# Transposing q on VectorE from the ninth item on, and moving tiles so that both operands of a matmul start at the same address modulo 512

## The chip, the cores and the metric

The kernel runs on one core of a Trainium2 chip. The metric is the device time of one execution in microseconds. The median of three runs before the change is 977.59 us (977.21 to 977.76).

## What is computed

Linear attention with two softmaxes, then a two-layer network with the Mish activation. The batch is 8, there are 8 heads, 576 positions and a head dimension of 64; the network has 4608 tokens, width 512 and inner width 2048. All in float32.

```python
q_s = softmax(q, axis=-1)            # over the 64 elements of a row
k_s = softmax(k, axis=2)             # over the 576 positions
kv  = einsum('bhsd,bhse->bhde', k_s, v)
att = einsum('bhsd,bhde->bhse', q_s, kv)
x   = att.transpose(0, 2, 1, 3).reshape(4608, 512)
h   = x @ w_in
out = (h * tanh(log1p(exp(h)))) @ w_out
```

## The kernel before

**Items.** Attention is done in 32 items, one for each batch `b` and pair of heads `hp`; an item's two heads fill the 128 rows of TensorE. An item gives one 128x512 slab of x transposed (`xs`, features on partitions), for the first 512 of the 576 positions. The last 64 positions of all items (`xt`) go through DRAM and make a ninth column of tokens at the end.

**Slots.** The network runs in slots. Slot n takes one column of 512 tokens (`c = n // 16`) and one block of 128 inner features (`f = n % 16`). `h_mm` makes `ph` of 12 matmuls: for each of the four 128-blocks of x, the weights are stationary and x is streamed, and each product is made of three with operands split in a high and a low part (`wih`, `wil`, and x's two halves). `act` applies Mish on ScalarE (`y`) and splits the result into `gh` and `gl` on VectorE. `out_mm` comes three slots later (LAG = 3) and adds to four accumulators `po` with 12 matmuls: `gh` and `gl` are stationary and `wo` is streamed. There are 144 slots, so 1728 ph and 1728 po matmuls.

**Order.** `group(n)` writes four slots (u = 0 to 3) and puts one attention item i between them, a batch ahead of its use. At u = 1 stand `a_kv` (pkv on TensorE), `a_qscale` (row sums `qs` on VectorE, scaling of `qe` on POOL) and `a_kvs` (kvbd and its split kvr); at u = 2 `a_qt` (q transposed) ahead of `out_mm`, and behind `act` the next item's maxima (`a_max`: kmx, then qm), `a_x` (px, pxt) and `a_split` (xs); at u = 3 `a_kmax1` (pk, mxd) and `a_kmax2` (pb) for the next item. Its exponentials and the load of the one after it end the group. From slot 20 on the order on TensorE, ScalarE, VectorE and POOL is that of the code. All loads and stores are issued by SP. The first four items and the weights' preparation make a prologue; weights are still converted until about 150 us, by VectorE, ScalarE and POOL.

**q before.** `a_load` puts q's 576 rows of a head on partitions, four neighbouring rows to a partition, as 2 x 5 x 64 elements (the fifth block is the tail, held twice). The row's maximum, sum and scaling are then over 64 elements within a partition. `a_qt` transposes with five matmuls by the identity into PSUM (pq four times, pqt once). ScalarE copies pq to `qT` (for items from 8 = COLS on as the high part, with VectorE's `qTl` the low part) and pqt to `qTt`. `a_x` multiplies kv with them: three products for the 512 positions from item 8 on, one for the tail.

**Addresses.** Tiles lie in pools, in the order of their allocation; tiles named gap only take up room. In the built program the start addresses within a partition, modulo 512 bytes, are:

| tiles | role | before | after |
|---|---|---|---|
| wih, wil | stationary in ph | 192 | 64 |
| xs | streamed in ph | 64 | 64 |
| gh, gl | stationary in po | 64 | 64 |
| wo | streamed in po | 64 | 64 |
| kvrh, kvrl | stationary in px | 128 | 64 |
| qT, from item 8 on (qTh in the changed kernel) | streamed in px | 320 | 320 |
| qTl | streamed in px | 64 | 64 |

Every slice that one of these matmuls reads starts a multiple of 512 bytes behind the start of its tile.

Of the kernel before, what the change touches and what calls it, by code (L numbers as in the profile page):

```python
# [8 lines left out]
F32 = mybir.dt.float32  # L9
F32R = mybir.dt.float32r  # L10
U32 = mybir.dt.uint32
AF = mybir.ActivationFunctionType
ALU = mybir.AluOpType
AX = mybir.AxisListType
P = 128
# [7 lines left out]


@with_exitstack
def attn_mish_mlp(ctx: ExitStack, tc: tile.TileContext, q, k, v, w_in, w_out, out):

    nc = tc.nc  # L30
    B, H, S, D = q.shape
    DM, DFF = w_in.shape
    HP = H // 2
    NC = 4
    SM = NC * P
# [6 lines left out]
    NITEM = B * HP  # L42
    START = 20
    COLS = 2 * HP
    ET = mybir.EngineType

    cp = ctx.enter_context(tc.tile_pool(name="cp", bufs=1))
    lp = ctx.enter_context(tc.tile_pool(name="lp", bufs=1))
    ap = ctx.enter_context(tc.tile_pool(name="ap", bufs=1))
    xp = ctx.enter_context(tc.tile_pool(name="xp", bufs=1))  # L50
    sp = ctx.enter_context(tc.tile_pool(name="sp", bufs=4))
# [10 lines left out]
    kvbd = [pool.tile([P, P], F32, tag="kvbd", name=f"kvbd{i}") for i, pool in enumerate((pp, cp))]  # L62
    for t in kvbd:
        nc.vector.memset(t, 0.0)
    kvr = [cp.tile([P, P], F32R, tag=f"kvr{x}", name=f"kvr{x}") for x in "hl"]
    cp.tile([P, 16], F32, tag="gap", name="gap0")
    wi = [cp.tile([P, HP, DFF], F32R, tag=f"wi{x}", name=f"wi{x}") for x in "hl"]


# [3 lines left out]
    def sub(eng, out, a, b):  # L73
        eng.tensor_tensor(out, a, b, ALU.subtract)  # L74
# [68 lines left out]
    def w_end(m):  # L143

        if m < -1:
            return max(0, m + 5)
        return max(4, 2 + sum(w_due(u) <= m + 3 for u in units))

    def w_step():
        j = wstep[0]  # L150
        wstep[0] += 1
        for i, stage in ((j - 1, w_hi), (j - 2, w_lo), (j + 2, w_abs), (j + 1, w_low), (j, w_bits)):
            if 0 <= i < len(units):
                stage(units[i])
        if j + WAHEAD < len(units):
            w_load(j + WAHEAD)

    def w_until(m):
        while wstep[0] < w_end(m):
            w_step()  # L160


    at = {}
    xs = {}
    ap.tile([P, 24], F32, tag="gap", name="gap1")
    xt_dram = dp.tile([B, P, HP, ST], F32, name="xt_dram")

    vt = [p.tile([P, 2, NC + 1, D + 2], F32, tag=f"v{j}", name=f"v{j}") for j, p in enumerate((pp, pp, pp, lp))]
# [6 lines left out]
    def a_load(i):  # L175
        if i >= NITEM:
            return
        b, hp = divmod(i, HP)
        hs = slice(2 * hp, 2 * hp + 2)
        r = at[i] = {}  # L180
        for nm, src in (("k", k), ("q", q)):
            t = (pp if i < 3 else lp).tile([P, 2, NC + 1, D], F32, tag=f"{nm}{min(i, 3)}", name=f"{nm}{i}")
            nc.sync.dma_start(t[:, :, 0:NC, :], src[b, hs, 0:SM, :].rearrange("h (p c) d -> p h c d", c=NC))
            tail = src[b, hs, SM:S, :].rearrange("h p d -> p h d")
            nc.sync.dma_start(t[0:ST, :, NC, :], tail)
            nc.sync.dma_start(t[ST:P, :, NC, :], tail)
            r[nm] = t
# [20 lines left out]
    def a_max(i):  # L208
        a_kmx(i)
        a_qm(i)  # L210

    def a_qm(i):
        if i >= NITEM:
            return
        r = at[i]
        qt = r["q"].rearrange("p h c d -> p (h c) d")
        qm = ap.tile([P, 2 * (NC + 1)], F32, tag="qm", name=f"qm{i}")
        nc.vector.tensor_reduce(qm, qt, axis=AX.X, op=ALU.max)  # L218
        sub(nc.gpsimd, qt, qt, qm.unsqueeze(2).to_broadcast([P, 2 * (NC + 1), D]))

    def psum(i, tag, name):

        if i < HP and tag != "a":
            return (ps_h if tag == "h" else ps_o).tile([P, 512], F32, tag=tag, name=name)
        return ps_a.tile([P, 512], F32, tag="a", name=name)
# [20 lines left out]
    def a_exp(i, which="kq"):  # L246
        if i >= NITEM:
            return
        r = at[i]
        for nm in which:  # L250
            e = (pp if i in (0, 2) else ap).tile([P, NC + 1, 2, D], F32, tag=f"{nm}e", name=f"{nm}e{i}")
            nc.scalar.activation(e.rearrange("p c h d -> p h c d"), r[nm], AF.Exp)  # L252
            r[nm + "e"] = e

    def a_kv(i):
# [4 lines left out]
        for c in range(NC + 1):  # L260
            if i >= COLS:
                for j in range(2):
# [7 lines left out]
    def a_qscale(i):  # L270
        if i >= NITEM:
            return
        q2 = at[i]["qe"].rearrange("p c h d -> p (c h) d")
        qs = ap.tile([P, 2 * (NC + 1)], F32, tag="qs", name=f"qs{i}")
        nc.vector.tensor_reduce(qs, q2, axis=AX.X, op=ALU.add)  # L275
        nc.vector.tensor_scalar_add(qs, qs, 1e-9)
        nc.vector.reciprocal(qs, qs)  # L277
        nc.gpsimd.tensor_tensor(q2, q2, qs.unsqueeze(2).to_broadcast([P, 2 * (NC + 1), D]), ALU.mult)  # L278

    def a_kvs(i):  # L280
        if i >= NITEM:
# [6 lines left out]
        for j in range(2):  # L288
            h = slice(j * D, (j + 1) * D)
            o = 0 if i >= COLS else j * (D + 2)  # L290
            if i < HP:
                nc.scalar.activation(bd[h, h], pkv[h, o:o + D], AF.Copy, scale=rs[h])
            else:
                nc.vector.tensor_scalar_mul(bd[h, h], pkv[h, o:o + D], rs[h])
        if i >= COLS:
            nc.vector.tensor_copy(kvr[0], bd)
            sub(nc.vector, kvr[1], bd, kvr[0].bitcast(F32))

    def a_qt(i):
        if i >= NITEM:  # L300
            return
        r = at[i]
        xr = i >= COLS
        pool = pp if i in (0, 2) else ap
        qT = pool.tile([P, SM], F32R if xr else F32, tag="qT", name=f"qT{i}")
        qTt = pool.tile([P, ST], F32, tag="qTt", name=f"qTt{i}")
        pq = psum(i, "o1", f"pq{i}")
        for c in range(NC):
            nc.tensor.transpose(pq[:, c * P:(c + 1) * P], r["qe"][:, c].rearrange("p h d -> p (h d)"), ident)  # L309
        nc.scalar.copy(qT, pq)  # L310
        if xr:
            qTl = sp.tile([P, SM], F32R, tag="wc", name=f"qTl{i}")
            sub(nc.vector, qTl, pq, qT.bitcast(F32))
            r["qTl"] = qTl
        pq2 = psum(i, "o2", f"pqt{i}")
        nc.tensor.transpose(pq2[:, 0:P], r["qe"][:, NC].rearrange("p h d -> p (h d)"), ident)
        nc.scalar.copy(qTt, pq2[:, 0:ST])
        r["qT"] = qT, qTt

    def a_x(i):  # L320
# [5 lines left out]
        px = psum(i, "o3", f"px{i}")  # L326
        if i >= COLS:
            nc.tensor.matmul(px, kvr[0], qT, start=True, stop=False)  # L328
# [70 lines left out]
    def evac(c, t, copy):  # L399
        ob = pools["wp"].tile([P, DM], F32, tag="w", name=f"ob{c}_{t}")  # L400
        copy(ob, po[t])
        if c < B:
            nc.sync.dma_start(out[c * S:c * S + SM, :].rearrange("(p c) e -> p c e", c=NC)[:, t, :], ob)
        else:
            nc.sync.dma_start(out.rearrange("(b s) e -> b s e", b=B)[2 * t:2 * t + 2, SM:S, :], ob)

    def group(n):
        i = HP + n // G
        for u in range(G):
# [3 lines left out]
            if u == 0 and NITEM <= i < NITEM + HP:  # L413
                t_load(i - NITEM)
            elif u == 1:
                a_kv(i)
                a_qscale(i)
                a_kvs(i)
                v_load(i + 1)
            elif u == 2:  # L420
                a_qt(i)
            elif u == 3:
                a_kmax1(i + 1)
            if 0 <= o < NSLOT:
                out_mm(o)
                if o % NF == NF - 1:
                    for t in range(NC):
                        evac(o // NF, t, nc.scalar.copy if t >= 2 or i >= NITEM else nc.vector.tensor_copy)
# [10 lines left out]
            elif u == 3:  # L439
                a_kmax2(i + 1)  # L440
        a_exp(i + 1)
        a_load(i + 2)

    def first_units():
        w_abs(units[0])
        w_abs(units[1])
        w_low(units[0])

    stages = dict(L=a_load, V=v_load, R=w_load, MK=a_kmx, MQ=a_qm, A=a_kmax1, B=a_kmax2,
                  EK=lambda i: a_exp(i, "k"), EQ=lambda i: a_exp(i, "q"), K=a_kv, Q=a_qscale,  # L450
                  S=a_kvs, T=a_qt, X=a_x, Z=a_split)
    with tc.manual_schedule(engines={ET.PE}):
        for token in PROLOGUE.split():
            name = token.rstrip("0123456789")
            if name == "C":
                first_units()
            else:
                stages[name](int(token[len(name):]))
        w_until(-1)
        start.__exit__(None, None, None)  # L460
        pools["wp"] = ctx.enter_context(tc.tile_pool(name="wp", bufs=7))
        pools["rp"] = ctx.enter_context(tc.tile_pool(name="rp", bufs=LAG + 1))
    for n in range(0, START, G):
        group(n)
    with tc.manual_schedule(engines={ET.Activation, ET.PE, ET.DVE, ET.Pool}):
        for n in range(START, NSLOT + LAG, G):
# [28 lines left out]
```

## Time and profile before

| | |
|---|---|
| median of three runs | 977.59 us |
| profiled execution, its own time | 976.49 us |
| its span | 974.6 us |
| mean granted TensorE clock | 0.974 |
| TensorE busy | 906.6 us, 93% |
| VectorE busy | 448.9 us, 46% |
| ScalarE busy | 313.5 us, 32% |
| GpSimd (POOL) busy | 174.5 us, 18% |

Busy times show which engine is full. The 40 slices of the span show when. The chain of waits, followed back from the last instruction, shows what ended last at each step. A row of the timeline has the start, the length, the engine, the line, the operation and its tiles, and in brackets how long the engine was idle before and what ended that. In the rows of the chain, the length runs until the next piece begins. Since matmuls are pipelined, TensorE's time is read best from the distance of such pieces.

### The profile page before, as it was taken

What the parts mean: (1) busy time and instruction counts of PE and PEld (TensorE: products, weight loads), DVE (VectorE), ACT (ScalarE), POOL (GpSimd) and SP (SyncE); (2) the same over time, 40 slices, a digit from 0 to 9 for tenths busy, and PEclk for the clock granted to TensorE, in tenths of its full rate; (3) what the DMA queues carried; (4) which work ended last, traced back from release to release, by engine and by line L of the source; (5) the groups of instructions that cost most, each with busy time, mean ns of one, the idle gap of its engine ahead of it and who ended that gap; (6) DMA issues with size and microseconds to landing.
All of it is one profiled execution on the core that took longest, in us unless ns stands there. A gap on an engine that the chain in (4) does not pass through costs nothing.

```text
span 974.6 us, 11611 instructions
## 1 busy us (share of the span) xinstructions
PE 906.6 (93%) x4392; PEld 726.5 (75%) x4392; DVE 448.9 (46%) x814; ACT 313.5 (32%) x504; POOL 174.5 (18%) x146
## 2 busy tenths in 40 slices
PE   3786869999999999999999999999999999999990
PEld 2565658888878887888878887888788888888880
DVE  6899985344444444544354444444544222221210
ACT  3675654523342333333333323322333121110100
POOL 4577775211111110100011111111111000000000
PEclk9898889999999999999999999999999999999995
DMA  6685421211121112111221112111210020010001
GB/s 167 197 266 169 130 99 41 84 28 41 41 84 41 41 41 84 41 41 40 64 61 41 41 42 84 41 41 41 84 41 2 13 66 11 0 44 1 1 1 43
DMA packets 98944, 59.49 MB, mean 61 GB/s; under 512 B 67656, under 2 KB 92232, under 8 KB 98888
## 3 DMA queue, kind: packets, MB, share of 16 engines
q1 hardware_dynamic: 98888, 58.75, 21.4%
q8 instruction: 35, 0.57, 0.2%
q14 instruction: 21, 0.17, 0.1%
HBM read 48.23 MB, written 10.49 MB: 60 GB/s over the span
## 4 chain that ended last, share of the span: by engine, by line
PE 85%; DVE 7%; POOL 2%; issue 2%; SPq 1%; ACT 1%; DMA 1%; POOLq 0%; ACTq 0%; DVEq 0%
PE po L396 39%; PE ph L373 39%; PE pkv L263 2%; PE pq L309 1%; DVE wc_out L113 1%; DVE wc_out L114 1%; DVE wc_in L113 1%; DVE raw_in L109 1%; DVE kmx L205 1%; PE px L330 1%; PE px L328 1%; PE px L329 1%; DVE wc_in L114 1%; PE pk L232 1%; PE pxt L334 0%
## 5 line engine op out<-in xcount | busy, mean ns | idle before, releaser
L373 PE MATMUL ph<-xs,wih 128*128 128x512 f32 x1152 | 371.5, 404 | 0.7 <-ACT xs L350 0.7
L396 PE MATMUL po<-wo,gh 128*128 128x512 f32 x1152 | 366.7, 399 | 0.0
L373 PEld LDWEIGHTS ph<-xs,wih 128*128 128x128 f32 x1152 | 215.4, 191 | 50.3 <-ACT xs L350 1.1
L396 PEld LDWEIGHTS po<-wo,gh 128*128 128x128 f32 x1152 | 211.5, 189 | 44.9
L373 PE MATMUL ph<-xs,wil 128*128 128x512 f32 x576 | 229.0, 398 | 1.2 <-POOL wil L74 1.2
L396 PE MATMUL po<-wo,gl 128*128 128x512 f32 x576 | 227.0, 394 | 0.0
L384 DVE CAST gh<-y 128x512 fp32r<-128x512 f32 x144 | 69.8, 485 | 267.0 <-ACT y L381 267.0
L381 ACT ACTIVATE y<-ph 128x512 f32<-128x512 f32 x144 | 86.5, 601 | 274.5 <-PE ph L373 252.3
L373 PEld LDWEIGHTS ph<-xs,wil 128*128 128x128 f32 x576 | 109.8, 191 | 27.3 <-POOL wil L74 1.6
L396 PEld LDWEIGHTS po<-wo,gl 128*128 128x128 f32 x576 | 108.6, 189 | 25.5
L74 DVE TENSOR_TENSOR gl<-y,gh 128x512 fp32r<-128x512 f32 x124 | 85.9, 693 | 6.6
L74 POOL TENSOR_TENSOR q<-q,qm 128x640 f32<-128x640 f32 x32 | 42.2, 1319 | 260.5 <-DVE qm L218 260.4
L278 POOL TENSOR_TENSOR qe<-qe,qs 128x640 f32<-128x640 f32 x32 | 41.0, 1282 | 264.2 <-DVE qs L277 202.8
L74 DVE TENSOR_TENSOR qTl<-pq,qT 128x512 fp32r<-128x512 f32 x24 | 16.6, 692 | 102.1 <-ACT qT L310 102.1
L310 ACT CAST qT<-pq 128x512 fp32r<-128x512 f32 x24 | 14.1, 587 | 153.4 <-PE pq L309 153.4
L252 ACT ACT_TABLE_LOAD x33 | 42.3, 1283 | 59.2 <-DVE k L244 58.9
L381 ACT ACT_TABLE_LOAD x34 | 43.6, 1283 | 4.8 <-PE ph L373 4.3
L205 DVE TENSOR_REDUCE kmx<-k 128x128 f32<-128x640 f32 x32 | 41.2, 1288 | 6.7 <-DMA k<-in_k_dram 6.7
L244 DVE TENSOR_TENSOR k<-k,pb 128x640 f32<-128x640 f32 x32 | 26.2, 818 | 25.9 <-PE pb L242 25.9
L74 POOL TENSOR_TENSOR gl<-y,gh 128x512 fp32r<-128x512 f32 x20 | 28.5, 1424 | 34.9 <-DVE gh L384 31.6
L350 ACT CAST xs<-px 128x512 fp32r<-128x512 f32 x32 | 18.8, 586 | 44.6 <-PE px L330 41.4
L275 DVE TENSOR_REDUCE qs<-qe 128x10 f32<-128x640 f32 x32 | 26.0, 814 | 6.2 <-ACT qe L252 5.4
(66 smaller groups left out, 618.0 us busy)
## 6 DMA issues: line engine op xcount, KB each, us to landing
out_dram<-ob SPq DMA_DIRECT2D x36, 256.0 KB, 2.5
k<-in_k_dram SPq DMA_DIRECT2D x32, 256.0 KB, 2.8
q<-in_q_dram SPq DMA_DIRECT2D x32, 256.0 KB, 3.1
raw_in<-in_moe_w_in_dram SPq DMA_DIRECT2D x16, 512.0 KB, 5.1
v<-in_v_dram SPq DMA_DIRECT2D x64, 128.0 KB, 2.9
raw_out<-in_moe_w_out_dram SPq DMA_DIRECT2D x16, 512.0 KB, 5.4
k<-in_k_dram SPq DMA_DIRECT2D x64, 32.0 KB, 2.5
q<-in_q_dram SPq DMA_DIRECT2D x64, 32.0 KB, 2.5
```

Of the source, the lines that this page charges most:

```text
L74: eng.tensor_tensor(out, a, b, ALU.subtract)
L113: nc.vector.scalar_tensor_tensor(a, a, 3, low, ALU.logical_shift_left, ALU.bitwise_or)
L114: nc.vector.scalar_tensor_tensor(a, high, 0x80000000, a, ALU.bitwise_and, ALU.bitwise_or)
L205: nc.vector.tensor_reduce(kmx, r["k"].rearrange("p h c d -> p h d c"), axis=AX.X, op=ALU.max)
L244: nc.vector.tensor_tensor(r["k"], r["k"], mb.unsqueeze(2).to_broadcast([P, 2, NC + 1, D]), ALU.subtract)
L252: nc.scalar.activation(e.rearrange("p c h d -> p h c d"), r[nm], AF.Exp)
L275: nc.vector.tensor_reduce(qs, q2, axis=AX.X, op=ALU.add)
L278: nc.gpsimd.tensor_tensor(q2, q2, qs.unsqueeze(2).to_broadcast([P, 2 * (NC + 1), D]), ALU.mult)
L373: nc.tensor.matmul(ph, wi[a][:, t, fs], x[:, z], start=t == 0 and i == 0, stop=t == HP - 1 and i == 2)
L381: nc.scalar.activation(y, ph, AF.Mish)
L384: nc.vector.tensor_copy(hi, y)
L396: nc.tensor.matmul(po[t], g[a][:, t * P:(t + 1) * P], wo[f][:, z], start=f == 0 and i == 0, stop=f == NF - 1 and i == 2)
```

## The change

For items 8 to 31, q comes in another layout. The inputs of the program get a second copy of q, `qs`, rearranged ahead of the launch without arithmetic: an item is 128 partitions of 576 elements, where a partition holds one of the two heads, one of the two halves of a row and one of 32 row numbers, and along the partition stand 18 blocks of 32 elements. It is loaded with one DMA instead of three.

A row of 64 is now in two partitions, 32 apart. So the maximum and the sum are made over 32 elements, and `halves` joins them: four copies swap neighbouring groups of 32 partitions into `sw`, and one operation combines the two. `a_qt` transposes each 32x32 block on VectorE in one instruction, which gives qT with the features of both heads on the partitions and the positions in their own order. ScalarE copies the first 512 positions as high part, VectorE makes the low part, and the tail is read by pxt from the transposed tile itself, which stands in ke's buffer. As the positions of q keep their order, the rows of the output of batches 2 to 7 are stored in runs of 128 neighbouring rows, not with a distance of four.

In the second part, gap tiles are changed and one added, so that wi and kvr move as the table shows.

```diff
+    cp.tile([P, 112], F32, tag="gap", name="gap0")
     kvr = [cp.tile([P, P], F32R, tag=f"kvr{x}", name=f"kvr{x}") for x in "hl"]
-    cp.tile([P, 16], F32, tag="gap", name="gap0")
...
-    ap.tile([P, 24], F32, tag="gap", name="gap1")
+    ap.tile([P, 40], F32, tag="gap", name="gap1")
...
+        if i >= COLS:
+            t = r["q"] = lp.tile([P, NB, 32], F32, tag="q3", name=f"q{i}")
+            nc.sync.dma_start(t, qs[i].rearrange("p (n f) -> p n f", f=32))
+        for nm, src in (("k", k), ("q", q))[:1 if i >= COLS else 2]:
...
+    def halves(st, op):
+        sw = ap.tile([P, NB], F32, tag="sw", name="sw")
+        for a in range(4):
+            nc.vector.tensor_copy(sw[32 * (a ^ 1):32 * (a ^ 1) + 32], st[32 * a:32 * a + 32])
+        nc.vector.tensor_tensor(st, st, sw, op)
...
+        if i >= COLS:
+            qt = r["q"]
+            qm = ap.tile([P, NB], F32, tag="qm", name=f"qm{i}")
+            nc.vector.tensor_reduce(qm, qt, axis=AX.X, op=ALU.max)
+            halves(qm, ALU.max)
+            sub(nc.gpsimd, qt, qt, qm.unsqueeze(2).to_broadcast([P, NB, 32]))
+            return
...
+        nc.vector.tensor_reduce(z, q2, axis=AX.X, op=ALU.add)
+        if i >= COLS:
+            halves(z, ALU.add)
...
+        if i >= COLS:
+            qT = ap.tile([P, S], F32, tag="ke", name=f"qT{i}")
+            nc.vector.transpose(qT, r["qe"].rearrange("p n f -> p (n f)"))
+            hi = ap.tile([P, SM], F32R, tag="qT", name=f"qTh{i}")
+            nc.scalar.copy(hi, qT[:, 0:SM])
+            lo = sp.tile([P, SM], F32R, tag="wc", name=f"qTl{i}")
+            sub(nc.vector, lo, qT[:, 0:SM], hi.bitcast(F32))
+            r["qTl"] = lo
+            r["qT"] = hi, qT[:, SM:S]
+            return
...
+        elif c < B:
+            nc.sync.dma_start(out[c * S + t * P:c * S + (t + 1) * P, :], ob)
...
+        ap.tile([P, 104], F32, tag="gap2", name="gap2")
```

How the order changes, at item 13. On TensorE, at u = 2, around the transposes and the po run of that slot; before:

```order
L373 MATMUL ph_2554<-xs_2195,wil 128x512
L309 MATMUL pq_2569<-ident,qe_2456 128x128 x4
L316 MATMUL pqt_2577<-ident,qe_2456 128x128
L396 MATMUL po_0_2429<-wo_668,gh_2447 128x512 x2
L396 MATMUL po_0_2429<-wo_668,gl_2448 128x512
```

and now:

```order
L406 MATMUL ph_2578<-xs_2212,wil 128x512
L429 MATMUL po_0_2449<-wo_669,gh_2467 128x512 x2
L429 MATMUL po_0_2449<-wo_669,gl_2468 128x512
L429 MATMUL po_1_2450<-wo_669,gh_2467 128x512 x2
L429 MATMUL po_1_2450<-wo_669,gl_2468 128x512
```

The po run now stands directly behind ph; px and pxt stand behind it as before.

On VectorE, from the end of u = 1 to u = 3, where `qTl` is the low part of q transposed, `qm` the row maxima of the next item, and `mxd` what TensorE's pb waits for; before:

```order
L74 TENSOR_TENSOR gl_2551<-y_2548,gh_2550 128x512
L74 TENSOR_TENSOR qTl_2575<-pq_2569,qT_2567 128x512
L384 CAST gh_2594<-y_2592 128x512
L74 TENSOR_TENSOR gl_2595<-y_2592,gh_2594 128x512
L205 TENSOR_REDUCE kmx_2598<-k_2458 128x128
L218 TENSOR_REDUCE qm_2600<-q_2462 128x10
L351 TENSOR_TENSOR xs_2609<-px_2603,xs_2609 128x512
L234 TENSOR_REDUCE mxd_2630<-pk_2628 128x1
```

and now:

```order
L76 TENSOR_TENSOR gl_2575<-y_2572,gh_2574 128x512
L333 STREAM_TRANSPOSE qT_2591<-qe_2476 128x576
L76 TENSOR_TENSOR qTl_2595<-qT_2591,qTh_2593 128x512
L417 CAST gh_2611<-y_2609 128x512
L76 TENSOR_TENSOR gl_2612<-y_2609,gh_2611 128x512
L210 TENSOR_REDUCE kmx_2615<-k_2480 128x128
L233 TENSOR_REDUCE qm_2617<-q_2478 128x18
L223 COPY sw<-qm_2617 32x18 x4
L224 TENSOR_TENSOR qm_2617<-qm_2617,sw 128x18
L384 TENSOR_TENSOR xs_2632<-px_2626,xs_2632 128x512
L255 TENSOR_REDUCE mxd_2653<-pk_2651 128x1
```

The transpose has come in ahead of qTl, and five small instructions ahead of the low half of xs and mxd.

More of the change, by code (lines that the diff above doesn't have):

```diff
@@ L25, in attn_mish_mlp @@
 @with_exitstack
-def attn_mish_mlp(ctx: ExitStack, tc: tile.TileContext, q, k, v, w_in, w_out, out):
+def attn_mish_mlp(ctx: ExitStack, tc: tile.TileContext, q, k, v, w_in, w_out, qs, out):
     nc = tc.nc
@@ L44, in attn_mish_mlp @@
     COLS = 2 * HP
+    NB = S // 32
     ET = mybir.EngineType
@@ L180, in a_load @@
         r = at[i] = {}
-        for nm, src in (("k", k), ("q", q)):
+        if i >= COLS:
+            t = r["q"] = lp.tile([P, NB, 32], F32, tag="q3", name=f"q{i}")
+            nc.sync.dma_start(t, qs[i].rearrange("p (n f) -> p n f", f=32))
+        for nm, src in (("k", k), ("q", q))[:1 if i >= COLS else 2]:
             t = (pp if i < 3 else lp).tile([P, 2, NC + 1, D], F32, tag=f"{nm}{min(i, 3)}", name=f"{nm}{i}")
@@ L250, in a_exp @@
         for nm in which:
+            if nm == "q" and i >= COLS:
+                e = r["qe"] = ap.tile([P, NB, 32], F32, tag="qe", name=f"qe{i}")
+                nc.scalar.activation(e, r["q"], AF.Exp)
+                continue
             e = (pp if i in (0, 2) else ap).tile([P, NC + 1, 2, D], F32, tag=f"{nm}e", name=f"{nm}e{i}")
@@ L272, in a_qscale @@
             return
[L273 to L278, printed above, removed]
+        q2 = at[i]["qe"] if i >= COLS else at[i]["qe"].rearrange("p c h d -> p (c h) d")
+        n, w = q2.shape[1:]
+        z = ap.tile([P, n], F32, tag="qs", name=f"qs{i}")
+        nc.vector.tensor_reduce(z, q2, axis=AX.X, op=ALU.add)
+        if i >= COLS:
+            halves(z, ALU.add)
+        nc.vector.tensor_scalar_add(z, z, 1e-9)
+        nc.vector.reciprocal(z, z)
+        nc.gpsimd.tensor_tensor(q2, q2, z.unsqueeze(2).to_broadcast([P, n, w]), ALU.mult)
     def a_kvs(i):
@@ L302, in a_qt @@
         r = at[i]
-        xr = i >= COLS
+        if i >= COLS:
[8 more added lines that the diff above has]
+            return
         pool = pp if i in (0, 2) else ap
-        qT = pool.tile([P, SM], F32R if xr else F32, tag="qT", name=f"qT{i}")
+        qT = pool.tile([P, SM], F32, tag="qT", name=f"qT{i}")
         qTt = pool.tile([P, ST], F32, tag="qTt", name=f"qTt{i}")
@@ L310, in a_qt @@
         nc.scalar.copy(qT, pq)
[L311 to L314, printed above, removed]
         pq2 = psum(i, "o2", f"pqt{i}")
@@ L401, in evac @@
         copy(ob, po[t])
-        if c < B:
+        if c < COLS // HP:
             nc.sync.dma_start(out[c * S:c * S + SM, :].rearrange("(p c) e -> p c e", c=NC)[:, t, :], ob)
+        elif c < B:
+            nc.sync.dma_start(out[c * S + t * P:c * S + (t + 1) * P, :], ob)
         else:
@@ L488 @@
     B, H, S, D = inputs['q'].shape
+    a = _np.ascontiguousarray(inputs['q'].reshape(B * H // 2, 2, S // 32, 32, 2, 32).transpose(0, 1, 4, 3, 2, 5))
+    arrays["in_qs_dram"] = a = a.reshape(B * H // 2, 128, S)
+    args.append(nc.dram_tensor("in_qs_dram", a.shape, _mybir.dt.float32, kind="ExternalInput").ap())
     DM = inputs['moe_w_out'].shape[1]
```

## Prediction

> **What bounds the kernel now.** I read the page's busy shares and slices first, then the chain of waits in order of time, then VectorE's timeline, since VectorE receives the moved work.
>
> ```profile
> span 974.6 us, 11611 instructions
> PE 906.6 (93%) x4392; PEld 726.5 (75%) x4392; DVE 448.9 (46%) x814; ACT 313.5 (32%) x504; POOL 174.5 (18%) x146
> PE   3786869999999999999999999999999999999990
> DVE  6899985344444444544354444444544222221210
> PEclk9898889999999999999999999999999999999995
> PE 85%; DVE 7%; POOL 2%; issue 2%; SPq 1%; ACT 1%; DMA 1%; POOLq 0%; ACTq 0%; DVEq 0%
> ```
>
> TensorE is the bound: it holds 85% of the chain that ended last. Its slices are full from the seventh on, where the clock is full too; ahead of that, up to about 150 us, VectorE is full and TensorE waits. So what leaves TensorE behind 150 us shortens the run one for one, and what leaves it earlier is mostly not seen. From there a group of four slots looks like this (chain of waits, start, length, line):
>
> ```profile
> 398.70 2.80 PE ph L373 x12
> 401.50 0.73 PE pkv L263 x20
> 402.24 2.97 PE po L396 x12
> 405.20 2.79 PE ph L373 x12
> 408.00 0.44 PE pq L309 x4
> 408.44 0.11 PE pqt L316
> 408.55 2.75 PE po L396 x12
> 411.29 0.23 PE px L328
> 411.53 0.23 PE px L329
> 411.76 0.24 PE px L330
> 411.99 0.17 PE pxt L334 x2
> 412.16 2.83 PE ph L373 x12
> 415.00 0.11 PE pk L232
> 415.11 2.77 PE po L396 x12
> 417.87 0.11 PE pb L242
> 417.98 2.79 PE ph L373 x12
> 420.77 2.76 PE po L396 x12
> ...
> 149.73 2.80 PE ph L373 x12
> ...
> 768.60 2.76 PE po L396 x12
> 771.36 2.80 PE ph L373 x12
> ...
> 940.75 10.92 PE po L396 x48
> ```
>
> Every piece stands on the end of the last; no other engine appears. A slot is 12 ph and 12 po matmuls; one attention item per group of four slots stands between them.
>
> **Part 1, the transposes leave TensorE.** Items 8 to 31 lose pq (0.44) and pqt (0.11). The po run behind them takes 2.75, no less than the 2.76 of one without them, so they hide nothing of each other: 0.55 x 24 items = 13.2 us, all behind 150 us and on the path. Bounds: 0 if something else fills the hole, 13.2 if nothing does. I take 13.2, because nothing else stands in these rows.
>
> **Part 2, what takes their place on VectorE.** The rows that matter there, of the same group and of one at the end of a batch (391 us), with one from the start (144 us):
>
> ```profile
> 400.08 0.22 DVE L277 RECIPROCAL qs<-qs 128x10 f32<-128x10 f32 x1
> 403.55 0.29 DVE L74 TENSOR_TENSOR kvrl<-kvbd,kvrh 128x128 fp32r<-128x128 f32 x1
> 404.22 0.69 DVE L74 TENSOR_TENSOR gl<-y,gh 128x512 fp32r<-128x512 f32 x1
> 409.14 0.69 DVE L74 TENSOR_TENSOR qTl<-pq,qT 128x512 fp32r<-128x512 f32 x1 [4.24 <-ACT qT L310]
> 412.04 0.81 DVE L218 TENSOR_REDUCE qm<-q 128x10 f32<-128x640 f32 x1
> 415.14 0.29 DVE L234 TENSOR_REDUCE mxd<-pk 128x1 f32<-128x128 f32 x1 [1.70 <-PE pk L232]
> ...
> 391.08 0.28 DVE L234 TENSOR_REDUCE mxd<-pk 128x1 f32<-128x128 f32 x1
> 392.89 0.27 PE L242 MATMUL pb<-ident,mxd 128*128 128x128 f32 x1
> ...
> 144.36 1.26 DVE L276 TENSOR_SCALAR qs<-qs 128x10 f32<-128x10 f32 x1
> ...
> 400.46 1.26 POOL L278 TENSOR_TENSOR qe<-qe,qs 128x640 f32<-128x640 f32 x1 [8.55 <-DVE qs L277]
> 408.53 0.59 ACT L310 CAST qT<-pq 128x512 fp32r<-128x512 f32 x1 [6.39 <-PE pq L309]
> ```
>
> The trace has no VectorE transpose. The nearest row is a pass over 640 elements, 0.81 us; the new one passes over 576, so 0.73 is the low end, and four passes over 640, 3.2, is my high end, an estimate. I take 0.8, being nearest to one pass. It can start once the gl at 404.22 has ended (404.9); POOL's scaling of qe ends at 401.7 now, and about 1 us later behind the extra small instructions, still ahead of 404.9. Then the ScalarE copy of the high part (0.59 from PSUM; from SBUF between this and twice it) and qTl (0.69) give 407.1 at 0.8 and 409.5 at 3.2, with 0.1 for the hand-overs. The px that reads them starts at 411.29, now 0.55 earlier, 410.74. Both ends fit, so the transpose costs nothing; its cover is the 4.24 us in which VectorE waited for the old qT, and TensorE waits only from 4.4 us per transpose on. Behind qTl wait gh and gl of the same slot, read three slots later. At the end of a batch the room is the same, since the output copies wait for the po that runs ahead of px.
>
> Two times per item, four copies over 32 partitions and 18 elements and one 128x18 operation are added. Nearest rows: 0.22 for 128x10 and 0.29 for 128x128; low end 0.1 (half of the first), high end the blocked 1.26 below. I take 0.2, so 1.0 us for five. The five on qs delay POOL's scaling, covered above. The five on qm are the sensitive ones: behind them on VectorE stand the low half of xs and then mxd, for which TensorE's pb waits. In a normal group mxd waited 1.70 us for pk and then had 417.87 - 415.43 = 2.4 us, 4.1 us of room in all; in the six groups that end a batch, mxd ended at 391.36 against pb at 392.89, 1.5 us. One microsecond fits into both. I charge 0.5 us in all, for the batch ends and for the start.
>
> The rest goes together: the two reduces, the exponential and POOL's two operations pass over 576 instead of 640 elements, ScalarE loses the copy of qTt, SP issues one load of q instead of three, and the output rows are written in another order by as many DMAs. All of these lie on engines that wait in the rows above; they cost and gain nothing. The order on SP changes only in that two issues per item are gone, so what stands behind them leaves earlier.
>
> **Part 3, the addresses.** In the built program the stationary wi slices start at 192 modulo 512 and the streamed x at 64; gh, gl and wo all start at 64. With the change wi starts at 64 also; po's tiles keep their relation. So ph would become what po is. The trace has a difference between them: ph 2.80 per 12, po 2.76. More telling is the last row: 48 po with no ph between. If its first twelve take the 2.76 of any other, the other 36 take 8.16, or 2.72 per 12 (226.7 ns each). So po reaches 2.72 only some way behind a ph. The px matmuls, whose kvr stands at 128 modulo 512 and whose streamed tiles at 320 and 64, take 0.23 to 0.24, as ph does. Three relations that differ are slow, the one that agrees is fast; that is a correlation over few tiles, not a proof.
>
> Upper end: from the row at 149.73 there are 131 ph runs (144 slots less 13). All ph at 2.72 saves 0.08, all po 0.04 per slot: 131 x 0.12 = 15.7. Lower end: nothing, or a loss if the relation were the wrong one: ph at the 2.83 of its worst row, 131 x 0.03 = +4. What I take: in the 32 slots behind the last item all of it, 32 x 0.12 = 3.8. In a group, po behind pkv takes 2.97 and po behind pk 2.77, and I leave those as they are; two undisturbed ph give 0.08 each, two ph behind px and pb half, two po 0.04 each: 0.32 x 24.75 groups = 7.9. Together 11.7, nearer to the upper end, as po in the last row shows what a long run of one relation does.
>
> By the Trainium skill, TensorE: Matmul & The Clock Gate, section "Step-by-step: what each phase is for", loading the next weights takes no read bandwidth from the running matmul, as the two operands have read ports of their own. By that rule the address would not matter, part 3 would be 0 and the sum 13.2 less 0.5. The po and ph rows speak against it, as the two differ in nothing else that I see but what they read and where; no run here shows the ports.
>
> **Sum.** -13.2 - 11.7 + 0.5 = -24.4 against the profiled execution, whose span is 974.6 and whose own time is 976.49. The median of the runs shown is 977.59, 1.1 above; the saving is subtracted from it: 953.2.
>
> **Rivals.** *The transposes alone.* The addresses make no difference: 977.6 - 13.2 + 0.5 = 964.9. For it: po and ph also differ in that po streams the same two tiles twelve times and ph eight tiles, and that could be the cause. Against it: two of the px matmuls stream one tile and are slow. Chance 0.29. It is also what the rule of the Trainium skill in part 3 would bring.
>
> *VectorE's small instructions stall pb, and the kernel is slower.* The row at 144.36 shows a small operation at 1.26 us where the later one of its kind takes about 0.2, beside a busy POOL. If each of the five on qm took 1.26, they would take 6.3: 2.2 us beyond the room in 18 groups and 4.8 in six, 68 us, and the time would be 977.6 - 24.4 + 68 = 1021. The forecast saving is used up where the five exceed the 4.1 us by x with 18 x + 6 (x + 2.6) = 24.4, so x = 0.37: from 0.9 us per instruction on. Against it: POOL's own operation on q waits for these five, and its other on qe ended ten microseconds before, so POOL is idle there. Chance 0.04. The Trainium skill, SBUF — State Buffer, section "SBUF: two separate sides", says that VectorE and GpSimd lock a shared port for whole instructions; the row at 144.36 agrees with it, and by it too an idle POOL blocks nothing.
>
> *A wait gives most of the first gain back.* The transpose takes over 4.4 us, or pk starts to wait for xs: the chain would show an engine other than PE in each group, at 0.5 us per item (12 us), with the addresses idle: 977. Chance 0.03.
>
> *The addresses hurt.* The loss of 4 us from part 3: 969. Chance 0.03.
>
> **How the numbers follow.** The forecast has 0.61: both parts, between 949 (15.7 instead of 11.7) and 960 (a third of part 3). The transposes alone, 963 to 967, have 0.29. The range 949 to 967 leaves out the rest, 0.10 at most, and the edges. A difference of under 0.2%, about 2 us, can't be told from no change. Faster: 0.61 + 0.29 + 0.03 = 0.93; within 0.2%: 0.03; slower: 0.04.
>
> **What would show it.** Right: in the changed profile no pq and pqt for late items; a group of the chain 0.8 to 0.9 shorter; 12 ph at 2.72 to 2.76; the slots without attention at 5.44 instead of 5.55; every piece from 188 us on still PE. The transpose near 0.8 us and the 32x18 copies near 0.2. Wrong: a ph run that still takes 2.80 (then the addresses do nothing), a pb that waits for mxd, or a px that waits for qTl.

## Result and profile after

The changed kernel takes 953.0 us (951.55 to 953.48, four runs) against 977.4 us: ratio 0.9749, 95% interval 0.9732 to 0.9766. In a later comparison it took 953.26 against 976.69 (0.9763, interval 0.9749 to 0.9776). The profiled execution took 951.55. The forecast was 953.2.

The page of the changed kernel, span, busy shares, VectorE's slices and the chain:

```profile
span 949.9 us, 11408 instructions
PE 880.2 (93%) x4272; PEld 711.6 (75%) x4272; DVE 508.9 (54%) x1078; ACT 312.2 (33%) x480; POOL 169.5 (18%) x146
DVE  5899987355556555655565556555655122212210
PE 84%; DVE 6%; POOL 2%; issue 2%; DMA 1%; ACT 1%; SPq 1%; ACTq 0%; POOLq 0%; DVEq 0%
```

VectorE has 60 us more to do, and its share of the chain has not grown. The chain of waits, one group and two free slots (start, length, line):

```profile
402.30 2.82 PE ph L406 x12
405.12 0.11 PE pk L253
405.23 2.77 PE po L429 x12
408.00 0.11 PE pb L263
408.11 2.77 PE ph L406 x12
410.87 2.72 PE po L429 x12
413.59 2.72 PE ph L406 x12
416.31 0.74 PE pkv L288 x20
417.05 2.92 PE po L429 x12
419.97 2.72 PE ph L406 x12
422.69 2.72 PE po L429 x12
425.41 0.23 PE px L361
425.64 0.23 PE px L362
425.86 0.23 PE px L363
426.09 0.17 PE pxt L367 x2
...
801.09 2.72 PE po L429 x12
803.81 2.72 PE ph L406 x12
```

pq and pqt are gone from these groups, and ph and po take 2.72 wherever no matmul of the attention stands directly ahead of them. From the first matmul of one ph run to that of the next, a free slot (one without attention) takes 5.440 us (5.553 before) and a group of four slots 23.96 (24.82 before). 24 x 0.86 + 31 x 0.113 = 24.1 of the 24.7 by which the span is shorter; the rest is start and end, which differ by a microsecond between runs of one kernel (the run of ph with which the last 131 begin started at 148.4 in one profile of the changed kernel and at 149.8 in another).

VectorE's timeline, the same part of a group (start, length, operation, idle time before):

```profile
396.07 0.77 DVE L333 STREAM_TRANSPOSE qT<-qe 128x576 f32<-128x576 f32 x1
397.53 0.69 DVE L76 TENSOR_TENSOR qTl<-qT,qTh 128x512 fp32r<-128x512 f32 x1 [0.69 <-ACT qTh L335]
...
402.53 0.71 DVE L223 COPY sw<-qm 32x18 f32<-32x18 f32 x4
403.28 0.18 DVE L224 TENSOR_TENSOR qm<-qm,sw 128x18 f32<-128x18 f32 x1
403.49 0.69 DVE L384 TENSOR_TENSOR xs<-px,xs 128x512 fp32r<-128x512 f32 x1
405.27 0.29 DVE L255 TENSOR_REDUCE mxd<-pk 128x1 f32<-128x128 f32 x1 [1.09 <-PE pk L253]
...
382.96 0.28 DVE L255 TENSOR_REDUCE mxd<-pk 128x1 f32<-128x128 f32 x1
```

The transpose takes 0.77, the five small instructions 0.96 from the start of the first to the start of the next. mxd still waits for pk in a normal group; at the end of a batch (382.96) it ends 0.6 us ahead of pb.

### The profile page after: what moved, and what is told of

It is laid out like the page before. It is cut to its first block, busy times and chain, and to the rows that moved or that the text cites. A ratio compares the mean times of both kernels' runs of the same rounds, so it can differ in the third digit from the quotient of the medians.

```text
span 949.9 us, 11408 instructions
## 1 busy us (share of the span) xinstructions
PE 880.2 (93%) x4272; PEld 711.6 (75%) x4272; DVE 508.9 (54%) x1078; ACT 312.2 (33%) x480; POOL 169.5 (18%) x146
## 4 chain that ended last, share of the span: by engine, by line
PE 84%; DVE 6%; POOL 2%; issue 2%; DMA 1%; ACT 1%; SPq 1%; ACTq 0%; POOLq 0%; DVEq 0%
PE po L429 40%; PE ph L406 39%; PE pkv L288 2%; DVE wc_out L116 1%; DVE wc_out L115 1%; DVE wc_in L115 1%; DVE raw_in L111 1%; DVE wc_in L116 1%; PE px L362 1%; PE px L361 1%; PE px L363 1%; DVE kmx L210 1%; PE pk L253 1%; DMA raw_out<-in_moe_w_out_dram 0%; PE pxt L367 0%
## 5 line engine op out<-in xcount | busy, mean ns | idle before, releaser
L406 PE MATMUL ph<-xs,wih 128*128 128x512 f32 x1152 | 365.5, 398 | 0.3 <-ACT xs L383 0.2
L406 PE MATMUL ph<-xs,wil 128*128 128x512 f32 x576 | 226.4, 393 | 1.2 <-POOL wil L76 1.2
L417 DVE CAST gh<-y 128x512 fp32r<-128x512 f32 x144 | 67.2, 467 | 291.5 <-ACT y L414 291.5
L406 PEld LDWEIGHTS ph<-xs,wil 128*128 128x128 f32 x576 | 109.0, 189 | 25.4 <-POOL wil L76 1.6
L306 POOL TENSOR_TENSOR qe<-qe,qs 128x576 f32<-128x576 f32 (+1 forms) x32 | 38.6, 1207 | 279.1 <-ACT y L414 196.2
L76 POOL TENSOR_TENSOR q<-q,qm 128x576 f32<-128x576 f32 (+1 forms) x32 | 39.9, 1248 | 232.2 <-issue 210.2
L335 ACT CAST qTh<-qT 128x512 fp32r<-128x512 f32 x24 | 14.9, 621 | 84.1 <-DVE qT L333 82.8
L265 DVE TENSOR_TENSOR k<-k,pb 128x640 f32<-128x640 f32 x32 | 26.1, 816 | 24.9 <-PE pb L263 24.8
L253 PE MATMUL pk<-ident,kmx 128*128 128x128 f32 x32 | 9.7, 303 | 20.8 <-DVE kmx L210 15.0
L434 ACT COPY ob<-po 128x512 f32<-128x512 f32 x24 | 14.1, 587 | 43.0 <-PE po L429 41.4
```

Of the source, the lines that this page charges most:

```text
L253: nc.tensor.transpose(pk[:, 0:P], r["kmx"].rearrange("p h d -> p (h d)"), ident)
L265: nc.vector.tensor_tensor(r["k"], r["k"], mb.unsqueeze(2).to_broadcast([P, 2, NC + 1, D]), ALU.subtract)
L306: nc.gpsimd.tensor_tensor(q2, q2, z.unsqueeze(2).to_broadcast([P, n, w]), ALU.mult)
L406: nc.tensor.matmul(ph, wi[a][:, t, fs], x[:, z], start=t == 0 and i == 0, stop=t == HP - 1 and i == 2)
L417: nc.vector.tensor_copy(hi, y)
```

## Experiments

**Each part alone.** The changed kernel with the old addresses of kvr and wi:

```diff
-    cp.tile([P, 112], F32, tag="gap", name="gap0")
     kvr = [...]
+    cp.tile([P, 16], F32, tag="gap", name="gap0")
...
-    ap.tile([P, 40], F32, tag="gap", name="gap1")
+    ap.tile([P, 136], F32, tag="gap", name="gap1")
```

> The changed kernel with kvr and wi back at their old places (wi at 192, kvr at 128 modulo 512); all other TensorE tiles stay. My theory: the two parts add up. The transposes alone are worth 24 x 0.55 = 13.2 us, so about 964 us against 977.4 (ratio 0.9865); 12 ph take 2.80 again, a free slot 5.55, a group of four slots 24.82 - 0.54 = 24.28. Rival (the faster matmuls come from the cleaner order, without transposes between ph and po, not from the addresses): the free slot stays at 5.44 and the time near 953.

965.41 us against 976.91, ratio 0.988 (0.9864 to 0.9896). The free slot is 5.553, a group 24.28. And the kernel before with the new addresses:

```diff
+    cp.tile([P, 112], F32, tag="gap", name="gap0")
     kvr = [...]
-    cp.tile([P, 16], F32, tag="gap", name="gap0")
...
-    ap.tile([P, 24], F32, tag="gap", name="gap1")
+    ap.tile([P, 56], F32, tag="gap", name="gap1")
```

> The kernel before, with gap tiles that put wi and kvr at 64 modulo 512; q as before. My theory: a free slot takes 5.44 instead of 5.55, a group 24.82 - 0.32 = 24.5, together 31 x 0.113 + 24 x 0.32 = 11.2 us less: about 966 us (ratio 0.9885). Rival (the addresses do nothing, the gain is the transposes'): 977, free slot 5.55.

966.39 us, ratio 0.9888 (0.9874 to 0.9902). The free slot is 5.440, a group 24.55. A free slot in the chain of the first, then of the second:

```profile
803.31 2.80 PE ph L406 x12
806.11 2.76 PE po L429 x12
```

```profile
801.73 2.72 PE ph L373 x12
804.45 2.72 PE po L396 x12
```

The ph and po runs follow the addresses and not the transposes. The parts are worth 11.5 and 10.5 us (differences of these medians). Per group they are 0.54 and 0.27, together 0.81 of the 0.86: the po run behind pqt stays unsteady as long as pqt stands there, so 0.05 needs both. (Unsteady: the steps, from the start of one matmul to that of the next, vary between 224 and 236 ns before they settle at 226.7.)

**The relation or the place?** All tiles from kvr on 128 bytes further:

```diff
-    cp.tile([P, 112], F32, tag="gap", name="gap0")
+    cp.tile([P, 144], F32, tag="gap", name="gap0")
```

> The changed kernel with kvr, wi and all tiles behind them 128 bytes further: wi, xs, wo, gh, gl at 192 modulo 512, kvr at 192, qTh at 448; ident and kvbd stay. If it is the relation of the two tiles that counts, nothing changes: free slot 5.44, 12 ph 2.72, one time within 949 to 954. If 64 is a good place in itself, both ph and po get slower, towards 2.80: free slot 5.55 to 5.6, 964 or more.

952.73 us in one run, free slot 5.440. It is the relation of the two tiles; 64 is no better a place than 192.

**Which distance?** In three kernels wi is moved alone (a gap tile of 64, 16 or 8 floats behind kvr; gap1 is made so much larger that every tile behind it moves by 512; the loaded k, q and v lie between the two and move with wi):

```diff
     kvr = [...]
+    cp.tile([P, 64], F32, tag="gap3", name="gap3")
...
-    ap.tile([P, 40], F32, tag="gap", name="gap1")
+    ap.tile([P, 104], F32, tag="gap", name="gap1")
```

> The changed kernel with wi at 320 modulo 512 and x at 64: 256 apart. In the changed kernel px streams a tile that lies 256 from kvr and steps at 227 ns all the same, so my theory is now that the places have to agree modulo 256, not 512: free slot 5.44 and a time near 953. Rival (modulo 512, as the change says): 12 ph take 2.80, free slot 5.55, time 964 to 966.

> The changed kernel with wi at 128 modulo 512 and x at 64: 64 apart, kvr as in the changed kernel. Theory (any distance that is no multiple of 256 is slow, and equally): free slot 5.55, about 964. Rival (the cost grows with the distance): between 5.44 and 5.55, near 5.50. Second rival (only modulo 64 counts): 5.44 and 953; the kernel before, 128 apart, speaks against it.

> The changed kernel with wi at 96 modulo 512 and x at 64: 32 apart. Theory (any distance that is no multiple of 256 is slow, and equally): free slot 5.55, about 964. Rival (the cost grows with the distance): 5.46 to 5.48 and 955 to 957.

| wi behind x, modulo 512 | free slot | group | time, us |
|---|---|---|---|
| 0 (changed kernel) | 5.440 | 23.96 | 953.0 |
| 256 | 5.440 | 23.96 | 953.27 |
| 32 | 5.527 | 24.21 | 960.79 |
| 64 | 5.547 | 24.27 | 963.07 |
| 128 (the first of the parts alone; kvr at its old place, too) | 5.553 | 24.28 | 965.41 |

The rows of 256, 32 and 64 are single runs on another chip, where the kernel before took 976.64. A slot in the chain, of 256 and of 32 bytes off:

```profile
805.51 2.72 PE ph L407 x12
808.23 2.72 PE po L430 x12
```

```profile
805.67 2.79 PE ph L407 x12
808.47 2.73 PE po L430 x12
```

So the places have to agree modulo 256, not 512. Neither theory on the other distances holds fully: the cost grows with the distance, but three quarters of it are there at 32 bytes already. Between 0 and 32 and beyond 128 nothing was tried, save 256, and in none of these runs was a streamed tile moved alone.

**The unsteady stretches.** The changed kernel with ident and kvbd at 64, too:

```diff
+    cp.tile([P, 112], F32, tag="gap", name="gap0")
     ident = cp.tile([P, P], F32, tag="ident", name="ident")
...
-    cp.tile([P, 112], F32, tag="gap", name="gap0")
     kvr = [...]
```

> The changed kernel with the same 448-byte gap ahead of ident and kvbd, so that these too start at 64 modulo 512 (before at 128); nothing else moves. In the changed kernel the ph run behind pxt (which reads kvbd), the po run behind pk and the ph run behind pb (which read ident) go through about ten unsteady matmuls, 0.10, 0.05 and 0.05 us over 2.72. Theory A (an unsteady stretch is what an operand at another place leaves behind): these three lose 0.04 to 0.05 each, the group falls from 23.96 to about 23.82 and the time by 24 x 0.14 = 3.3 us, to about 949.7 (ratio to the kernel before 0.9715). Rival B (the unsteady stretch comes from the short matmuls whatever their addresses): no change, 953.

953.0 us, ratio 0.9757 (0.9739 to 0.9774); group 23.97. The chain reads as in the changed kernel behind pxt, pk and pb:

```profile
403.66 2.83 PE ph L406 x12
406.49 0.11 PE pk L253
406.60 2.77 PE po L429 x12
```

Theory A predicted a shorter group and falls: the stretch stays when kvbd and ident are moved. For pk nothing is left of it, since the other operand, kmx, starts at 320 in the built program and so both agree modulo 256; the tail of qT (32, read by pxt) and mxd (416, read by pb) keep places that don't agree. That short matmuls as such bring the stretch doesn't hold either. In the changed kernel the po run behind pkv, 20 short matmuls, goes evenly from its second step on. The third and the twelfth matmul of the po run behind pk and of the one behind pkv (TensorE's timeline):

```profile
405.53 0.40 PE L429 MATMUL po<-wo,gl 128*128 128x512 f32 x1
407.61 0.39 PE L429 MATMUL po<-wo,gl 128*128 128x512 f32 x1
...
417.54 0.39 PE L429 MATMUL po<-wo,gl 128*128 128x512 f32 x1
419.58 0.39 PE L429 MATMUL po<-wo,gl 128*128 128x512 f32 x1
```

Nine steps take 2.08 us behind pk and 2.04 behind pkv, 231 and 226.7 ns each. What makes the difference stays open.

**How much room VectorE has.** The transpose four times, then nine times over, always to the same place (the run with nine was made first, and what was expected of four builds on it):

```diff
-            nc.vector.transpose(qT, r["qe"].rearrange("p n f -> p (n f)"))
+            for _ in range(4):    # 9 in the other
+                nc.vector.transpose(qT, r["qe"].rearrange("p n f -> p (n f)"))
```

> The changed kernel with each VectorE transpose done four times: 3 x 0.81 = 2.4 us more. The run with nine showed TensorE waiting 2.4 us for 6.5 us more, so the room is 4.1 us. Theory: all hidden, 953 as in the changed kernel, no wait of px for qTh or qTl. Rival (part of a transpose's time reaches TensorE by another way, so that a fraction of any addition is paid): 24 x 2.4 us x that fraction; a tenth would be 6 us, 959.

951.69 us in one run, group 23.96, no wait on TensorE from 180 us to 900. Hidden whole.

> The changed kernel with each item's VectorE transpose done nine times over, to the same place. In the changed kernel one takes 0.77 us, and from the end of qTl to the third px there are 3.5 us. Theory (the transpose is hidden by that room and nothing else): eight more add 5.8 to 6.2 us, TensorE waits 2.4 to 2.7 us in each of 24 groups for qTl, 58 to 65 us in all, time 1011 to 1018. Rival (what the transposes delay, gh and gl or the maxima, reaches TensorE later by another way, too): more than 75 us. Rival (room beyond that which the rows show): under 40 us.

1032.87 us in one run, 80 more than the changed kernel. What TensorE waited for from 200 us to 900 (total, times, longest), pieces of the chain, and two stretches with busy times of PE, PEld, DVE, ACT, POOL, the granted clock, the DMA share and GB/s:

```profile
PE px L362 <- ACT qTh L336: 51.0, 23, 2.4
```

```profile
405.20 0.80 PE px L362
406.00 0.43 PE px L363
...
433.19 0.50 PE px L362
433.69 0.23 PE px L363
```

```profile
500.00:600.00 100.00, 91.38 (x440) 72.55 (x438) 73.20 (x155) 24.74 (x38) 8.12 (x7) 0.93 0.16 47
800.00:900.00 100.00, 97.79 (x447) 80.18 (x446) 32.64 (x63) 19.58 (x32) 1.16 (x1) 1.00 0.08 22
```

The wait itself is as expected: 2.4 us for qTh, and 0.4 more in the steps of px, whose third matmul waits for qTl. So groups take 26.7, 2.75 longer, and 23 of them lose 63 us. But 13 of the 23 took 27.9 or more, 1.2 to 1.6 us beyond that, and one of these 2.9; there lies the rest of the 80. Behind their waits, as at 405, the clock was granted at half for 3.4 us (once for 6.8), and matmuls of 512 columns started 427 ns apart instead of 227. So neither rival is the reason why more than 75 us were lost; it is the clock.

**The sensitive path, mxd to pb.** The five small instructions on qm four times over:

```diff
-            halves(qm, ALU.max)
+            for _ in range(4):
+                halves(qm, ALU.max)
```

> The changed kernel with the joining of the row maxima (four copies of 32x18 and one 128x18 operation) done four times instead of once, which gives the same maxima: 15 more small instructions ahead of xs and mxd, 3 x 0.93 = 2.8 us. Theory (the room for pb that the rows show is all there is): in a normal group mxd has 1.09 us of waiting and 2.4 us to pb, 3.5 us, so nothing is seen; at the end of a batch mxd ends 0.6 us ahead of pb, so TensorE waits 2.1 us for mxd in each of the six such groups, 13 us, time 966. Rival (VectorE is behind everywhere): 2 us or more in all 24 groups, 1000 or more. Rival (hidden everywhere): 953.

971.06 us in one run. TensorE's only wait from 180 us to 900, and a stretch behind one of them with the columns as above:

```profile
PE pb L264 <- DVE mxd L256: 10.7, 5, 2.2
```

```profile
292.00:296.00 4.00, 4.00 (x12) 3.13 (x13) 2.14 (x3) 1.75 (x2) 0.43 (x1) 0.60 0.00 0
```

Five waits of 2.1, each at the end of a batch, and none in the other groups: the rows gave the room rightly. The expectation counted six ends of a batch; the first, in slots 16 to 19, shows no wait. VectorE's order is not yet that of the code there: in the changed kernel's timeline kmx, qm and the five instructions don't stand between the output copies and mxd in that group. By the starts of ph, the five groups take 26.55 instead of 24.20, 11.8 us together. The clock adds to it: three of the waits were followed by 3.4 us at half clock, and the groups behind them took 25.4 to 25.6 instead of 23.96, 4.6 us together. That is 16.4 of the 18 us lost; the rest is not traced to a group.

**Fewer interruptions.** kmx earlier and pk directly ahead of px:

```diff
             elif u == 2:
                 a_qt(i)
-            elif u == 3:
-                a_kmax1(i + 1)
...
+            if u == 2:
+                a_kmax1(i + 1)
             if m < NSLOT:
                 act(m)
             w_until(m)
-            if u == 2:
-                a_max(i + 1)
+            if u == 1:
+                a_kmx(i + 1)
+            elif u == 2:
+                a_qm(i + 1)
```

> The changed kernel with the next item's kmx made at u = 1, ahead of the transpose, and pk put directly ahead of px at u = 2 instead of between ph and po at u = 3. TensorE is then interrupted four times per group, not five. Theory (each interruption costs TensorE the long first step of 314 ns and some 45 ns of unsteady matmuls behind it, whatever its addresses): a group loses 0.04 to 0.13 us, 24 x that is 1 to 3 us, and the wait of pk for kmx at the end of a batch (0.2 us, six times) goes: 949.5 to 951.5 against 953 for the changed kernel. Rival (px behind pk is unsteady as long as po was): only the 1.2 us of the batch ends, 951.8.

954.3 us (0.9781, interval 0.9762 to 0.98), beside the changed kernel in the same comparison:

> The changed kernel as it is, beside the run with pk moved, so that the two are compared on one chip: 953 by all theories.

953.26 us (0.9763). The chain of the moved kernel:

```profile
405.45 0.11 PE pk L253
405.56 0.23 PE px L361
...
406.42 2.81 PE ph L406 x12
409.22 2.72 PE po L429 x12
```

The po run of u = 3 falls to 2.72, a group to 23.91, and no group at the end of a batch is longer than another: 2.2 us less over 23 groups. But the last 131 ph runs begin at 152.9 instead of 149.8 us, so the 3.1 us lost in the start take more than the gain. What TensorE waited for from 85 us to 155 (total, times, longest), and the chain at the second of these waits:

```profile
PE pxt L367 <- DVE mxd L255: 7.8, 2, 4.0
...
137.49 1.64 DVE wc_out L116
...
139.15 0.30 DVE mxd L255
...
139.50 0.69 PE pxt L367 x2
```

In the new order pxt takes the PSUM buffer that pk had two tiles earlier (`ps_a` has two buffers), so it waits until mxd has read pk, and mxd stands behind VectorE's conversion of the weights. TensorE's waits in this stretch add up to 20.4 us, against 16.6 in the changed kernel beside it. Moving pk only for the groups behind the start was not tried. The profile of the moved kernel shows a granted clock of 0.95 from 144 us to 932, where that of the changed kernel beside it shows 1.0; its free slot is 5.440 all the same. No kernel here beats the changed one beyond its interval.

## Why the prediction was right

*The transposes leave TensorE, 13.2 us.* Right: 0.54 per group in the run of this part alone, 13.0 over 24 items; by the times 11.5, with an interval of about 10 to 13. The 13.2 was read from chain rows rounded to 0.01.

*VectorE takes the transpose and the small instructions at no cost.* Right, with the durations near those taken from the nearest rows: 0.77 (0.8 forecast), 0.18 (0.2). The room for the transpose was put at 4.4 us in all. With nine, one after another every 0.81 us, 6.5 us were added and a group took 2.75 longer: so some 3.75 can be added to one, 4.5 in all, close to the forecast. (The 4.1 us of the fourfold run's expectation are the room up to the wait for qTh alone.) The room of mxd at the end of a batch was put at 1.5 us; 0.6 is left behind the five instructions, and the added work of the fourfold run came out as a wait of 2.1, as these rows say. The prediction counted six groups with this shorter room; there are five.

*The addresses, 11.7 us.* Right in the sum: 0.32 per group and 0.113 per free slot, 24 x 0.32 + 31 x 0.113 = 11.2 on top of the transposes. Wrong in where: the ph behind px got 0.01 and the ph behind pb 0.02, where 0.04 each was forecast, while the po behind pkv, which was left as it was, got 0.05, from 2.97 to 2.92. And the place that must agree was taken as modulo 512 from the change's own words. The trace of the changed kernel spoke against it at once: px streams qTh at 320 against kvr at 64, and its three steps take 0.68 us (from 425.41 to 426.09), 227 ns each, where they took 0.70 before (from 411.29 to 411.99). The run at 256 settles it. The forecast's slower edge, "960 (a third of part 3)", comes to 961 if the third is one of 11.7; nothing hangs on it.

*The Trainium skill's rule.* By the Trainium skill, TensorE: Matmul & The Clock Gate, section "Step-by-step: what each phase is for", the two operands' read ports are independent. The kernel before with nothing but tiles moved gains 10.5 us, so here the place of the stationary tile against the streamed one does matter, and the measurement decides. The runs don't show where in the chip the two meet.

*0.5 us for waits.* Nothing of it can be told from the spread of the start. No rival came true.

*How near it came.* 953.2 against 953.0 is luck in part: runs of the changed kernel alone lie between 951.55 and 953.48, and the two parts were worth 22.0 by their own runs, not the 24.9 that were forecast for them. What needs both, 0.05 in each of 24 groups or 1.2 us, was not in the sum.

## What to carry to other kernels

Where TensorE's chain has no gaps, read the distance between matmuls by kind: two kinds of one shape that differ (here 2.80 and 2.76 per 12, and 2.72 in a long run of one kind) say that something in their operands costs time, and the tiles' start addresses modulo 256 are one cheap thing to try. Work is free on another engine only within the room that its rows show, the shortest in any of the groups; five small instructions on the path to a short matmul had 1.5 us there and a transpose about four and a half. Past that room, the price was more than the wait.

## What was not expected of the hardware

The distance of 512-column matmuls whose weights change each time is 226.7 ns when stationary and streamed tile start at the same place modulo 256, and about 233 on average at 32 to 128 bytes off (2.79 to 2.80 per 12). Behind pk, pb and pxt, which are short, some ten matmuls are unsteady (224 to 236 ns) before the distance settles; behind pkv, short too, they are not. A ph run with addresses 128 apart doesn't settle within its 12 matmuls (steps of 228 to 241 ns).

A wait of TensorE of 2.1 to 2.4 us was enough, in 13 of 23 cases and in 3 of 5, for the clock to be granted at half for 3.4 us (once for 6.8); each time but that one it cost some 1.2 to 1.6 us beyond the wait. In the changed kernel, without such waits, the granted clock is full from 137 us to 928.
